# Four filler memsets of the logits, moved ahead of the logits in a column-normalised attention with a soft mixture of experts

## The chip, the cores and the metric

The kernel runs on one core of one Trainium2 chip. The metric is the device time of one execution in microseconds (us), as the median of the runs.

## The reference, cut to what matters

q, k and v are 4 batches of 5056 rows by 256 columns, all float32.

```python
qn = q / (np.linalg.norm(q, axis=1, keepdims=True) + 1e-06)
kn = k / (np.linalg.norm(k, axis=1, keepdims=True) + 1e-06)
s = kn.transpose(0, 2, 1) @ qn / tau          # 256 x 256 for each batch
a = softmax(s, axis=-1)
x = (v @ a).reshape(20224, 256)
logits = x @ phi                              # 20224 rows, 32 slots
d = softmax(logits, axis=0)                   # over all rows
slot_input = d.T @ x                          # 32 x 256
slot_out = relu(slot_input @ w1[e]) @ w2[e]   # 8 experts, 4 slots each
out = softmax(logits, axis=1) @ slot_out
```

## The kernel before

The core has four engines that compute: TensorE (PE) multiplies matrices into PSUM, which has eight banks (here S0, S1, T0, T1, LB, GB, X0, X1); VectorE (DVE) and ScalarE (ACT) read and write PSUM and SBUF; GpSimd (POOL) does little here. All loads and stores are issued by SyncE (SP), in one queue. Each engine works through its own list of instructions in order, and waits for others by semaphores.

**The attention, in steps of 512 rows.** A step u (0 to 39, ten for each batch) loads 512 rows of q and k into the tile `raw` (five buffers). ACT squares them (`sq`, L206) and makes a rounded copy (`hl`, `cast`, L185); DVE computes the rounding's remainder (`low`, L191) and adds up the squares (L212). PE adds the products of k and q to two banks (`S`, L227, L233, L234). When a batch is done, ACT and DVE take `S` out (`shi` L242, `ssb` L247), DVE folds the sums of squares (`att_sums`, L251), PE adds them over the partitions (`nn`, L257), DVE copies the result (`rn`, L262), and the softmax follows. The result, multiplied by `phi`, is `M`, 256 by 32.

**The logits, in pieces of 1024 rows of v.** A piece p (0 to 19, five for each batch) is loaded as `v` and transposed (`vt`, by a second load or by PE as `vTp` and an ACT copy). `logits(p, lb)` multiplies `vt` by `M` into the bank `lb` as the tile `L`: 128 partitions by 8 groups of 32 slots (L390). ACT copies `L` to `lt` (L412, `logit_copy`), DVE takes its maxima (`mxs`, L418) and a 32 by 32 transpose (`nat`, L422). After each group of three or two pieces the running maximum is found: PE turns it (`rp`, L433), DVE reduces it to one row (`row` L439, `rowrun` L442 or L444), PE spreads it over the partitions again (`cp`, L448), DVE copies it out (`negm`, L453), ACT takes the exponential of `lt` (L469), DVE transposes that to `dn` (L479), and PE gathers `dn` times `v` (`G`, L499). The pieces of one batch are worked on while PE and DVE are in the attention steps of the next batch.

**The filler.** A batch has 5056 rows and its last piece (p = 4, 9, 14, 19) only 960. Of its eighth group of rows the upper 64 partitions have no data. They are set to a large negative number, so that maxima and sums pass over them; the matmuls of that piece leave them alone:

```python
        if q == PB - 1:
            dve.memset(L[HD:, 7, :], -1e30)
```

This memset is inside `logits`, so it stands on DVE at the place where the step `logits` has in the list, and the first matmul of that step waits for it.

**The order.** Each piece of work is a step: `at(key, f, ...)` and `tail(...)` append it to a plan, and the table `ORDER` lists the numbers of the steps in the order in which they are emitted. It sets the order on every engine and in SP's queue. A tile that takes over a bank or a buffer waits for the last users of the tile that had it before.

Of the kernel before, what the change touches and what calls it, by code (L numbers as in the profile page):

```python
# [16 lines left out]
P, S, G = 128, 32, 4  # L17
UB = 10
PB = 5
# [9 lines left out]


ORDER = [
# [47 lines left out]
]  # L79


# [1 line left out]
def colnorm_attention_soft_moe(  # L83
# [27 lines left out]
    def bank(i, name):  # L111
        return ps.tile([P, 512], F32, tag=f"b{i}", name=name)
# [264 lines left out]
    XT = {17: sqtag[NU - 2], 18: sqtag[NU - 1], 19: sqtag[NU - UB]}  # L377
    Ls = {}

    def logits(p, lb):  # L380
        b, q = divmod(p, PB)
        M = st[b]["M"]
        L = bank(lb, f"L{p}")[:, : 8 * S].rearrange("p (j s) -> p j s", s=S)
        if q == PB - 1:
            dve.memset(L[HD:, 7, :], -1e30)
        for m in range(2):
            x = vts[p, m].rearrange("p (j w) -> p j w", w=P)
            for g in range(G):
                n = 7 if q == PB - 1 and g >= 2 else 8
                pe.matmul(  # L390
                    L[S * g : S * g + S, :n, :],
                    M[:, m, :],
                    x[:, :n, S * g : S * g + S],
                    start=m == 0,
                    stop=m == 1,
                )
        Ls[p] = L

    def group(p):
        b, q = divmod(p, PB)  # L400
# [356 lines left out]
        else:  # L757
            sp.dma_start(oa[b, p][:, hf], o2[:, hf])

    def wake(k):  # L760
        w = bank(X0, "wake")
        for _ in range(k):
            pe.matmul(w[:, :P], ones, ones, start=True, stop=True)

# [44 lines left out]
    for p in range(14):  # L809
        k = FV + 2 * p  # L810
        k += 0.5 if k % UB == UB - 1 else 0
        at(k, logits, p, (LB, T1)[p % 2])
        at(k + 0.25, logit_copy, p)
        at(k + 0.40, logit_max, p)
# [89 lines left out]
    for m in range(2):  # L904
        tail(0.35 + 0.3 * m, att_join, 3, m)
        tail(0.4 + 0.3 * m, att_scale, 3, m)
        tail(0.6 + 0.3 * m, att_exp, 3, m)
        tail(2.5 + 0.6 * m, att_turn, 3, m)
    tail(0.5, logits, 14, LB)
    tail(2.3, logit_max, 14)  # L910
    tail(2.3, logit_nat, 14)
# [21 lines left out]
    chain(2.8, 2, gl, 1)  # L933
    ts = {15: (5.3, S0), 16: (6.2, S1), 17: (9.1, LB), 18: (17.0, S0), 19: (18.0, S1)}
    for p, (t, lb) in ts.items():
        tail(t, logits, p, lb)
        tail(t + 1.0, logit_copy, p)
        tail(t + 1.0, logit_max, p)
        tail(t + (1.1 if p < 17 else 3.0), logit_nat, p)
# [133 lines left out]
```

## Time and profile before

| what | value |
|---|---|
| median of 3 runs | 295.02 us (294.59 to 295.24) |
| the profiled execution's own time | 296.7 us |
| its span, from the first instruction to the last | 294.8 us |
| busy: DVE, PE, ACT | 239.4, 255.5, 185.6 us |
| instructions: DVE, PE, ACT | 396, 2296, 268 |
| moved by DMA | 115.59 MB, 392 GB/s over the span |
| mean granted TensorE clock | 0.952 of 2.4 GHz |

The busy times are sums over the whole span; the ends of matmuls are modelled, so a busy PE is not PE at its peak. The profiled execution's time is 1.9 us more than its span; those 1.9 us lie before the first and behind the last instruction that the profile has.

### The profile page before, as it was taken

To read this page: it belongs to the slowest core of one execution; us is meant where nothing else is said; L and a number is where in the kernel's file an instruction comes from. 1 tells how busy PE (TensorE), PEld (TensorE's weight loads), DVE (VectorE), ACT (ScalarE), POOL (GpSimd) and SP (SyncE) were. 2 spreads that over 40 slices of the span, in tenths; PEclk is the share of its full clock that TensorE was granted. 3 is DMA by queue.
4 is the path that set the end of the run, shared out by engine and by line. 5 is a ranking of instruction groups with operands and counts; after the bars stand their busy time and mean duration, and the time that the engine had idled before them with its cause. 6 is when DMAs were issued, how large, how long until landed. Compare 5 with 4: busy or idle time off the path is not lost.

```text
span 294.8 us, 5824 instructions
## 1 busy us (share of the span) xinstructions
PE 255.5 (87%) x2296; PEld 196.3 (67%) x2296; DVE 239.4 (81%) x396; ACT 185.6 (63%) x268; POOL 5.6 (2%) x10
## 2 busy tenths in 40 slices
PE   5789999999989999997999999899999999986000
PEld 3679878878858888774877777566553778755000
DVE  1399999999999899999799999979975769996100
ACT  2898879968887876867657986146442435864200
POOL 0000001000001000000200000010000000000000
PEclk9999999999997999999999999999997999999555
DMA  7999999999999789999989999999999939999996
GB/s 253 411 422 414 422 424 421 418 425 403 403 396 391 271 311 419 417 423 422 425 328 399 412 414 421 420 420 422 418 415 418 412 133 385 412 417 421 420 427 275
DMA packets 23067, 115.59 MB, mean 392 GB/s; under 512 B 2688, under 2 KB 2688, under 8 KB 15104
## 3 DMA queue, kind: packets, MB, share of 16 engines
q1 hardware_dynamic: 23040, 115.22, 96.3%
q8 instruction: 18, 0.29, 0.4%
q14 instruction: 9, 0.07, 0.1%
HBM read 94.24 MB, written 20.97 MB: 391 GB/s over the span
## 4 chain that ended last, share of the span: by engine, by line
PE 42%; DVE 23%; DMA 15%; issue 9%; ACT 5%; SPq 1%; ACTq 0%; DVEq 0%
DVE sq L212 12%; PE S L227 11%; PE S L233 6%; DMA w<-in_moe_w_dram 6%; DVE hl L191 5%; PE G L499 5%; DMA out_dram<-o 5%; PE L L390 4%; DMA raw<-in_qk_dram 3%; PE S L234 3%; PE op L726 2%; PE op_None L726 2%; PE O L687 2%; DMA v<-in_v_dram 2%; PE vTp L368 2%
## 5 line engine op out<-in xcount | busy, mean ns | idle before, releaser
L227 PE MATMUL S<-raw 128*128 128x256 f32 (+1 forms) x328 | 85.2, 396 | 6.1 <-DMA raw<-in_qk_dram 5.7
L212 DVE TENSOR_TENSOR sq<-sq,sq 128x1024 f32<-128x1024 f32 (+1 forms) x63 | 84.9, 1368 | 1.4 <-ACT sq L206 0.8
L206 ACT ACTIVATE sq<-raw 128x2048 f32<-128x2048 f32 x40 | 76.1, 1913 | 13.6 <-DMA raw<-in_qk_dram 6.0
L227 PEld LDWEIGHTS S<-raw 128*128 128x128 f32 (+1 forms) x328 | 59.8, 195 | 17.8 <-DMA raw<-in_qk_dram 7.3
L233 PE MATMUL S<-hl 128*128 128x512 f32 x156 | 65.1, 447 | 0.6 <-DVE hl L191 0.6
L191 DVE TENSOR_TENSOR hl<-raw,hl 128x1024 fp32r<-128x1024 f32 x39 | 47.2, 1216 | 10.1 <-ACT hl L185 10.1
L234 PE MATMUL S<-hl 128*128 128x256 f32 x156 | 43.8, 281 | 0.0
L185 ACT CAST hl<-raw 128x1024 fp32r<-128x1024 f32 x39 | 40.1, 1044 | 5.8 <-PE S L234 2.0
L233 PEld LDWEIGHTS S<-hl 128*128 128x128 f32 x156 | 29.5, 189 | 9.2 <-issue 2.4
L234 PEld LDWEIGHTS S<-hl 128*128 128x128 f32 x156 | 29.6, 190 | 0.8
L750 DVE COPY o<-op_None 128x512 f32<-128x512 f32 x30 | 18.8, 681 | 7.5 <-DMA out_dram<-o 6.4
L748 ACT COPY o<-op_None 128x512 f32<-128x512 f32 x30 | 15.9, 593 | 12.2 <-DMA out_dram<-o 7.3
L499 PE MATMUL G<-v,dn 128*32 128x256 f32 (+1 forms) x320 | 23.3, 382 | 0.0
L726 PE MATMUL op_None<-so,cT 32*128 32x256 f32 x240 | 18.8, 397 | 2.6 <-DVE o L750 1.6
L390 PE MATMUL L<-vt,M 128*32 128x256 f32 (+1 forms) x272 | 17.4, 380 | 4.1 <-issue 2.8
L726 PEld LDWEIGHTS op_None<-so,cT 32*128 32x128 f32 x240 | 14.8, 184 | 6.2 <-PE op_None L726 3.1
L499 PEld LDWEIGHTS G<-v,dn 128*32 128x32 f32 (+1 forms) x320 | 11.8, 109 | 7.2 <-issue 1.8
L390 PEld LDWEIGHTS L<-vt,M 128*32 128x32 f32 x272 | 8.4, 109 | 10.2 <-issue 4.2
L368 PE MATMUL vTp<-ident,v 128*128 128x128 f32 x96 | 14.8, 280 | 0.0
L368 PEld LDWEIGHTS vTp<-ident,v 128*128 128x128 f32 x96 | 11.9, 145 | 2.5 <-issue 0.7
L412 ACT COPY lt<-L 128x256 f32<-128x256 f32 x20 | 7.1, 372 | 9.7 <-DVE mxs L418 5.2
L375 ACT COPY vt<-vTp 128x512 f32<-128x512 f32 (+1 forms) x18 | 10.5, 581 | 3.6 <-PE vTp L368 3.6
(113 smaller groups left out, 264.2 us busy)
## 6 DMA issues: line engine op xcount, KB each, us to landing
raw<-in_qk_dram SPq DMA_DIRECT2D x39, 1024.0 KB, 8.8
v<-in_v_dram SPq DMA_DIRECT2D x40, 512.0 KB, 8.7
out_dram<-o SPq DMA_DIRECT2D x15, 1024.0 KB, 13.2
vt<-in_vt_dram SPq DMA_DIRECT2D x21, 512.0 KB, 8.6
w<-in_moe_w_dram SPq DMA_DIRECT2D x8, 1024.0 KB, 12.2
w<-in_moe_w_dram SPq DMA_DIRECT2D x16, 512.0 KB, 10.0
out_dram<-o SPq DMA_DIRECT2D x10, 512.0 KB, 4.6
vt<-in_vt_dram SPq DMA_DIRECT2D x4, 480.0 KB, 9.3
```

Source lines behind the costliest of these rows:

```text
L185: act.copy(hl[:, :ns, 0::2, :], raws[u][:, :ns])
L191: dve.tensor_tensor(hl[:, :ns, 1::2, :], raws[u][:, :ns], hl[:, :ns, 0::2, :].bitcast(F32), op=ALU.subtract)
L206: act.activation(sq, raws[u], AF.Square)
L212: dve.tensor_tensor(a[:, lo:hi], a[:, lo:hi], s[:, lo:hi], op=ALU.add)
L227: pe.matmul(sm[:, :C], raw[:pc, j, 1, cols], raw[:pc, j, 0, :], start=first, stop=False, skip_group_check=True)
L233: pe.matmul(sm, hl[:, j, 2, cols], rhs, start=first, stop=False, skip_group_check=True)
L234: pe.matmul(sm[:, :C], hl[:, j, 3, cols], hl[:, j, 0, :], start=False, stop=False, skip_group_check=True)
L368: pe.transpose(tp[:, n : n + pc], vs[p][:pc, 4 * h + jj, P * m : P * m + P], ident[:pc, :pc])
L390: pe.matmul(L[S * g : S * g + S, :n, :], M[:, m, :], x[:, :n, S * g : S * g + S], start=m == 0, stop=m == 1,)
L499: pe.matmul(gp[S * g : S * g + S, :C], dn[:pc, x, j, :], vt[:pc, j, :], start=x == 0 and j < G, stop=x == n - 1 and j >= G,)
L726: pe.matmul(ops[b, p, hf, g][:, h, :], cT[b][S * g : S * g + S, 4 * i : 4 * i + 4, :].rearrange("s j t -> s (j t)"), so[S * g : S * g + S] ...
L750: dve.tensor_copy(dst, src)
```

## The change

The memset becomes a step of its own, `logit_fill`, which also takes the bank; `logits` takes the bank itself only where no such step did. The four new steps are put into the plan, and `ORDER` has each of them 10 to 14 places ahead of the `logits` of the same piece. Every number in the table at or above the first new step's is shifted by one for each new step below it; apart from that the order of the other steps is the same. `wake` gets a second parameter that no call uses.

```diff
+    def logit_bank(p, lb):
+        Ls[p] = bank(lb, f"L{p}")[:, : 8 * S].rearrange("p (j s) -> p j s", s=S)
+
+    def logit_fill(p, lb):
+        logit_bank(p, lb)
+        dve.memset(Ls[p][HD:, 7, :], -1e30)
+
     def logits(p, lb):
         b, q = divmod(p, PB)
         M = st[b]["M"]
-        L = bank(lb, f"L{p}")[:, : 8 * S].rearrange("p (j s) -> p j s", s=S)
-        if q == PB - 1:
-            dve.memset(L[HD:, 7, :], -1e30)
+        if p not in Ls:
+            logit_bank(p, lb)
+        L = Ls[p]
...
-        Ls[p] = L
...
         k += 0.5 if k % UB == UB - 1 else 0
+        if p % PB == PB - 1:
+            at(k - 0.9, logit_fill, p, (LB, T1)[p % 2])
         at(k, logits, p, (LB, T1)[p % 2])
...
+    tail(0.4, logit_fill, 14, LB)
     tail(0.5, logits, 14, LB)
...
     for p, (t, lb) in ts.items():
+        if p % PB == PB - 1:
+            tail(t - 0.1, logit_fill, p, lb)
         tail(t, logits, p, lb)
```

Of the table one line of each kernel, with the step of the filler of p = 4 (434) and that of its logits (434 before, 435 now):

```diff
-    188, 627, 387, 165, 557, 421, 187, 184, 628, 416, 388, 422, 561, 423, 559, 558, 630, 194, 562, 175, 429, 434,
+    188, 629, 387, 165, 559, 421, 187, 434, 184, 630, 416, 388, 422, 563, 423, 561, 560, 632, 194, 564, 175, 429,
```

In the rows below a name's first number is the piece, step or batch and the number behind the last underscore that of the buffer; DMAHW is a load, Activation is ACT, and a wait for DVE on DVE, or for PE on PE, is for an earlier instruction of the same engine.

**VectorE at the first filler (p = 4, at the turn from batch 1 to batch 2 of the attention).** Before:

```order
L191 TENSOR_TENSOR hl20_670<-raw20_655,hl20_670 128x4x256 [waits DMAHW6_49,Activation_49]
L422 STREAM_TRANSPOSE nat0_112<-L1_545 128x256
L251 TENSOR_TENSOR sq10_340<-sq10_340 128x1024
L439 TENSOR_REDUCE row0_0_706<-rp0_0_703 1x32 [waits PE_49]
L442 COPY rowrun_118<-row0_0_706 1x128 [waits DVE_49]
L247 TENSOR_TENSOR ssb1_710<-shi1_692,S1_0_371 128x256 [waits Activation_49]
L251 TENSOR_TENSOR sq10_340<-sq10_340 128x512
L385 MEMSET L4_728 64x32
L247 TENSOR_TENSOR ssb1_710<-shi1_692,S1_1_372 128x256 [waits Activation_49]
L191 TENSOR_TENSOR hl21_714<-raw21_664,hl21_714 128x4x256 [waits DMAHW0_49,Activation_49]
```

Now:

```order
L192 TENSOR_TENSOR hl20_670<-raw20_655,hl20_670 128x4x256 [waits DMAHW6_49,Activation_49]
L386 MEMSET L4_697 64x32 [waits DVE_49]
L429 STREAM_TRANSPOSE nat0_112<-L1_545 128x256
L252 TENSOR_TENSOR sq10_340<-sq10_340 128x1024
L446 TENSOR_REDUCE row0_0_708<-rp0_0_705 1x32 [waits PE_49]
L449 COPY rowrun_118<-row0_0_708 1x128 [waits DVE_49]
L248 TENSOR_TENSOR ssb1_712<-shi1_692,S1_0_371 128x256 [waits Activation_49]
L252 TENSOR_TENSOR sq10_340<-sq10_340 128x512
L248 TENSOR_TENSOR ssb1_712<-shi1_692,S1_1_372 128x256 [waits Activation_49]
L192 TENSOR_TENSOR hl21_716<-raw21_664,hl21_716 128x4x256 [waits DMAHW0_49,Activation_49]
```

The memset has moved up past six instructions, to just behind `hl20`, and waits there only for earlier work of DVE itself.

**VectorE at the second filler (p = 9, at the turn from batch 2 to batch 3).** Before:

```order
L428 TENSOR_REDUCE mx1_0_1189<-mxs1_0_1069 128x1 [waits DVE_49]
L251 TENSOR_TENSOR sq20_681<-sq20_681 128x512 [waits DVE_49]
L191 TENSOR_TENSOR hl30_1164<-raw30_1072,hl30_1164 128x4x256 [waits DMAHW6_49,Activation_49]
L608 TENSOR_SCALAR cs0_1108<-cs0_1108 128x40
L609 RECIPROCAL cs0_1108<-cs0_1108 128x40 [waits DVE_49]
L439 TENSOR_REDUCE row1_0_1205<-rp1_0_1199 1x32 [waits PE_49]
L444 TENSOR_TENSOR rowrun_118<-rowrun_118,row1_0_1205 1x128 [waits DVE_49]
L247 TENSOR_TENSOR ssb2_1210<-shi2_1191,S2_0_750 128x256 [waits Activation_49]
L551 COPY acc_116<-sp0_1186 32x256
L385 MEMSET L9_1213 64x32 [waits Activation_49]
L247 TENSOR_TENSOR ssb2_1210<-shi2_1191,S2_1_751 128x256 [waits Activation_49]
L453 COPY negm1_0_1243<-cp1_0_1241 128x1 [waits PE_49]
```

Now:

```order
L435 TENSOR_REDUCE mx1_0_1189<-mxs1_0_1069 128x1 [waits DVE_49]
L252 TENSOR_TENSOR sq20_681<-sq20_681 128x512 [waits DVE_49]
L386 MEMSET L9_1195 64x32 [waits Activation_49]
L192 TENSOR_TENSOR hl30_1164<-raw30_1072,hl30_1164 128x4x256 [waits DMAHW6_49]
L615 TENSOR_SCALAR cs0_1108<-cs0_1108 128x40
L616 RECIPROCAL cs0_1108<-cs0_1108 128x40 [waits DVE_49]
L446 TENSOR_REDUCE row1_0_1207<-rp1_0_1201 1x32 [waits PE_49]
L451 TENSOR_TENSOR rowrun_118<-rowrun_118,row1_0_1207 1x128 [waits DVE_49]
L248 TENSOR_TENSOR ssb2_1212<-shi2_1191,S2_0_750 128x256
L558 COPY acc_116<-sp0_1186 32x256
L248 TENSOR_TENSOR ssb2_1212<-shi2_1191,S2_1_751 128x256 [waits Activation_49]
L460 COPY negm1_0_1243<-cp1_0_1241 128x1 [waits PE_49]
```

The memset has moved up past seven instructions, ahead of `hl30`, and it has taken its wait for ACT along: the bank that `L9` takes was that of `L7`, which ACT copies to `lt` (L412). The waits for ACT of `hl30` and of the first `ssb` are gone, being covered by the memset's.

**TensorE at the same place** (further matmuls of the same tiles are left out). Before:

```order
L433 MATMUL rp1_0_1199<-ident_90,mx1_0_1189 1x128 [waits DVE_49]
L390 MATMUL L9_1213<-vt9_0_1172,M1_1003 32x256 [waits DMAHW5_49,DVE_49,PE_49]
L390 MATMUL L9_1213<-vt9_1_1147,M1_1003 32x256 [waits DMAHW3_49]
L390 MATMUL L8_1224<-vt8_0_1126,M1_1003 32x256 [waits DMAHW2_49]
L390 MATMUL L8_1224<-vt8_1_1162,M1_1003 32x256 [waits Activation_49]
L448 MATMUL cp1_0_1241<-negone_97,rowrun_118 128x1 [waits PE_49]
L257 MATMUL nn2_1248<-ones_95,sq20_681 128x1 x4
L227 MATMUL S3_0_1254<-raw30_1072 128x256 [waits DMAHW6_49]
```

Now:

```order
L440 MATMUL rp1_0_1201<-ident_90,mx1_0_1189 1x128 [waits DVE_49]
L398 MATMUL L9_1195<-vt9_0_1172,M1_1003 32x256 [waits DMAHW5_49,DVE_49,PE_49]
L398 MATMUL L9_1195<-vt9_1_1147,M1_1003 32x256 [waits DMAHW3_49]
L398 MATMUL L8_1224<-vt8_0_1126,M1_1003 32x256 [waits DMAHW2_49]
L398 MATMUL L8_1224<-vt8_1_1162,M1_1003 32x256 [waits Activation_49]
L455 MATMUL cp1_0_1241<-negone_97,rowrun_118 128x1 [waits DVE_49,PE_49]
L258 MATMUL nn2_1248<-ones_95,sq20_681 128x1 [waits DVE_49]
L258 MATMUL nn2_1248<-ones_95,sq20_681 128x1 x3
L228 MATMUL S3_0_1254<-raw30_1072 128x256 [waits DMAHW6_49]
```

The order of the matmuls is the same. The first of `L9` still waits for DVE, now for the memset at its new place; `cp` and `nn`, which came behind a matmul that had waited for a later DVE instruction, now have waits for DVE of their own, on `rowrun` and on the folded squares.

At the third filler (p = 14) the memset moves up past six DVE instructions and waits for no other engine, and at the fourth (p = 19) it moves up past four and waits for ACT's copy of `L16`, whose bank it takes.

## Rows read from the trace of the kernel before

**Rows 1.** The page: the engines' busy time; GB/s in 40 slices of the span.

```profile
PE 255.5 (87%) x2296; PEld 196.3 (67%) x2296; DVE 239.4 (81%) x396; ACT 185.6 (63%) x268; POOL 5.6 (2%) x10
...
GB/s 253 411 422 414 422 424 421 418 425 403 403 396 391 271 311 419 417 423 422 425 328 399 412 414 421 420 420 422 418 415 418 412 133 385 412 417 421 420 427 275
```

**Rows 2.** The chain that ended last: start us, us, what ("issue" is waiting).

```profile
85.84 0.84 issue
...
137.49 1.93 issue
```

**Rows 3.** What DVE waited for, 80 to 170 us: total us, times, longest.

```profile
DVE negm L453 <- PE cp L448: 2.0, 1, 2.0
DVE ssb L296 <- PE rq L289: 1.1, 1, 1.1
```

**Rows 4.** Timeline, first filler: start us, us, what, [idle before <- releaser].

```profile
85.80 0.67 DVE L251 TENSOR_TENSOR sq<-sq 128x512 f32<-128x512 f32 x1
...
86.49 0.09 DVE L385 MEMSET L<- 64x32 f32 x1
...
86.68 1.06 PE L390 MATMUL L<-vt,M 128*32 128x256 f32 x16 [0.84 <-issue]
...
88.89 1.72 PE L227 MATMUL S<-raw 128*128 128x256 f32 x4
89.06 0.16 DVE L262 COPY rn<-nn 128x4 f32<-128x4 f32 x1 [1.04 <-PE nn L257]
```

**Rows 5.** Timeline, second filler.

```profile
133.97 0.37 ACT L412 COPY lt<-L 128x256 f32<-128x256 f32 x1 [4.07 <-DVE mxs L418]
...
135.74 0.69 DVE L251 TENSOR_TENSOR sq<-sq 128x512 f32<-128x512 f32 x1
...
136.35 1.22 DVE L191 TENSOR_TENSOR hl<-raw,hl 128x1024 fp32r<-128x1024 f32 x1
...
136.87 0.39 ACT L412 COPY lt<-L 128x256 f32<-128x256 f32 x1
...
138.27 0.28 DVE L444 TENSOR_TENSOR rowrun<-rowrun,row 1x128 f32<-1x128 f32 x1
...
139.23 0.09 DVE L385 MEMSET L<- 64x32 f32 x1
...
139.42 1.92 PE L390 MATMUL L<-vt,M 128*32 128x256 f32 x32 [1.94 <-issue]
...
141.27 0.38 PE L448 MATMUL cp<-negone,rowrun 1*128 1x1 f32 x2
...
141.68 0.16 DVE L453 COPY negm<-cp 128x1 f32<-128x1 f32 x1 [2.05 <-PE cp L448]
...
142.49 2.84 PE L227 MATMUL S<-raw 128*128 128x256 f32 x12
```

**Rows 6.** Timeline, third filler.

```profile
186.24 1.13 PE L499 MATMUL G<-v,dn 128*32 128x256 f32 x16
...
188.42 0.09 DVE L385 MEMSET L<- 64x32 f32 x1
...
188.56 1.06 PE L390 MATMUL L<-vt,M 128*32 128x256 f32 x16 [1.20 <-DVE L L385]
...
189.73 1.20 DVE L191 TENSOR_TENSOR hl<-raw,hl 128x1024 fp32r<-128x1024 f32 x1
...
192.20 0.16 DVE L262 COPY rn<-nn 128x4 f32<-128x4 f32 x1 [0.60 <-PE nn L257]
```

**Rows 7.** Timeline, fourth filler.

```profile
209.41 0.37 ACT L412 COPY lt<-L 128x256 f32<-128x256 f32 x1 [1.83 <-DVE nat L422]
```

**Rows 8.** Stretches: us, busy of each engine, granted clock, DMA share, GB/s.

```profile
86.00:89.00 3.00, 2.32 (x27) 1.81 (x28) 2.02 (x4) 1.83 (x2) 0.00 (x0) 1.00 1.01 416
89.00:93.00 4.00, 4.00 (x14) 3.31 (x14) 3.90 (x8) 3.29 (x4) 1.01 (x1) 0.57 1.02 415
```

**Rows 9.** What SP's queue waited for, 82 to 112 us.

```profile
SPq L121 <- PE S L227: 18.9, 5, 7.4
```

More of the change, by code (lines that the diff above doesn't have):

```diff
@@ L758, in store, with wake @@
             sp.dma_start(oa[b, p][:, hf], o2[:, hf])
-    def wake(k):
-        w = bank(X0, "wake")
+    def wake(k, tb=X0):
+        w = bank(tb, "wake")
         for _ in range(k):
```

91 rows, old and new, of the table ORDER are left out of this document.

## The prediction

> **What bounds the kernel now.** I read the page first. Over the span PE is busy for 87%, and the loads run at 400 to 425 GB/s in most slices, with dips to 271, 311 and 328 GB/s in slices 14, 15 and 21 [rows 1]. A slice is 7.4 us, so the dips lie at 96 to 111 us and 147 to 155 us. No single engine carries the span, and the place has to be looked at by itself.
>
> The chain of waits comes next. Through the middle of the span it runs mostly on PE, and it holds two long pieces in which PE waits for nothing that the profile names: 0.84 us at 85.84 and 1.93 us at 137.49 [rows 2]. The timeline says what stands there. At 86.49 and at 139.23 DVE runs the filler memset, and PE's next matmul, `L`, starts 0.19 us later each time [rows 4, 5]. PE's order at the second place shows that this matmul waits for DVE. The same happens at 188.42, where the profile does name the memset as the releaser of a PE wait of 1.20 us [rows 6]. At the fourth filler PE does not wait for it, since it has `L18` to do first.
>
> Last the list of waits on DVE, from 80 to 170 us. The two longest entries are 2.0 us for `cp` and 1.1 us for `rq` [rows 3]; the wait of 1.04 us for `nn` is in the timeline [rows 4]. The waits for `cp` and `nn` lie just behind the two fillers: PE waits for DVE's memset, and then DVE waits for PE. Between these places DVE has hardly a gap, so what the change gives is what DVE gets of its own idle time there, more than what PE gets.
>
> **The first filler (p = 4).** DVE's work at 85.80 ends at 86.47, the memset at 86.58, `L4` starts at 86.68 [rows 4]. Now the memset stands six instructions earlier, behind `hl20`, and `L4` can start when `L3` is out, 0.84 us earlier. Behind it stand `cp` (needs `rowrun`, long done) and `nn` (needs the squares folded by 86.47, and reaches PE at about 87.1). Both move by the whole 0.84 us, and so does the S matmul of 88.89. DVE waited 1.04 us for `nn` until 89.06, so it takes all 0.84 us and still waits 0.2. The memset, 0.09 us, is only moved. **Term: 0.84 us.**
>
> **The second filler (p = 9).** PE waited 1.94 us, until 139.42 [rows 5]. Here the memset carries a wait for ACT's copy of `L7`, which ends at 136.87 + 0.39 = 137.26. DVE comes to the memset at 135.74 + 0.69 = 136.43, so it now stands still for some 0.85 us and starts `hl30` at about 137.35 instead of 136.35. Queued behind it on DVE are `hl30`, the two `cs`, `row`, `rowrun` and the two `ssb`, all about 1.0 us later; `rowrun`, which ended at 138.27 + 0.28 = 138.55, is what PE's `cp` then waits for. On PE `L9` starts at about 137.5, `L9` and `L8` take 141.27 - 139.42 = 1.85 us, to 139.4; `cp` waits for `rowrun` until 139.6 and `nn` follows; the S matmul starts at about 140.8 instead of 142.49, 1.67 us earlier. On DVE the second `ssb` ends at about 140.5, `cp` is already there, and `negm` starts at 140.5 instead of 141.68. So DVE gets back 1.18 us of its 2.05 us of idle time, and loses the rest to the new wait. I take DVE's figure, rounded, because DVE is dense afterwards. **Term: 1.15 us.** The bounds are 0, if the copy of `L7` is late by as much as the gain, and PE's 1.67 us.
>
> The Trainium skill, PSUM — Partial Sum Buffer, section "Engine vs sequencer instructions", says that the queues of ScalarE, VectorE and GpSimd are strictly first in, first out. By that rule nothing behind the memset can pass it while it waits for ACT, which is the 1.15 us above; if `hl30` could pass it, the term would be the whole 2.05 us. The rule speaks against moving a memset ahead of its bank's last reader, and no row of before shows this very wait.
>
> **The third filler (p = 14).** PE's gather ends at 186.24 + 1.13 = 187.37, and `L14` starts at 188.56 [rows 6]. The memset now stands six DVE instructions earlier and waits for no other engine. PE then does `L14`, the gather of piece 11 and the S matmuls of `hl38` and `hl39` about 1.1 us earlier; the last of these are held by the remainder of `hl39`, which DVE finishes at 189.73 + 1.20 = 190.9. DVE waited 0.60 us for `nn` before 192.20. From there to the end the chain goes through PE and short DVE pieces, so I take PE's value. **Term: 1.1 us,** bounds 0 (if the loads have become the limit here, where GB/s shows no dip) and 1.2.
>
> **The fourth filler (p = 19).** ACT's copy of `L16` waited for a transpose of DVE just ahead of the memset's new place, and then took 0.37 us, to 209.78 [rows 7]. DVE now waits there for most of that copy, and `cT`, `negm` and with it ACT's exponentials are later by up to 0.3 us, less the 0.09 us that fall away behind them. PE has `L18` to do meanwhile. **Term: -0.1 us,** bounds -0.3 and 0.
>
> **What follows the moved work.** No load changes its place in SP's queue. In the first dip that queue waits five times for PE's S matmuls, 18.9 us in all, to free `raw` buffers [rows 9]; earlier S matmuls issue those loads earlier and fill the dips. The two dips hold about (420-271 + 420-311 + 420-328)/420 x 7.4 = 6 us of load time, more than the 2 us that the first two terms ask of them.
>
> **The sum.** 0.84 + 1.15 + 1.1 - 0.1 = 3.0 us. The span goes from 294.8 to 291.8 us and the profiled execution's own time from 296.7 to 293.7. The median, 295.02 us, is 1.7 us below that execution, and I take the same 3.0 us from it: **292.0 us.** With all terms at their ends the sum lies between 0.5 us (0.84, 0, 0, -0.3) and, with the clock below, 4.8 us (0.84 + 1.1, 1.67, 1.2, 0).
>
> **Rivals.** *The clock comes along.* Right after the first pause and the narrow matmuls of `nn`, the granted clock falls: 1.00 from 86 to 89 us, a mean of 0.57 from 89 to 93 [rows 8]; 0.43 x 4.0 = 1.7 us of PE's time is lost to the 1.2 GHz level. Without the pause PE has wide matmuls in its place, and the clock might stay at 2.4 GHz. For: the fall follows on the pause. Against: after the longer pause at 137.49 PE goes on at 2.4 GHz, with 12 S matmuls in 2.84 us where 4 took 1.72 us after the first [rows 4, 5], so the pause alone does not decide. DVE could then also take its 1.1 us wait for `rq` [rows 3]: 295.02 - 4.1 = 290.9 us.
>
> *Half of it is eaten.* The copy of `L7` is ACT's and need not move with DVE, and the loads from 155 us on run without a dip. If only the first place pays, plus a little, the time is 294.0 us.
>
> *The loads set the time.* Then earlier compute only waits for data, and nothing changes: 295.0 us. For: 33 of the 40 slices are above 390 GB/s [rows 1]. Against: SP's queue waits for PE in the dips, and in the list of DVE's waits no load appears. The Trainium skill, Perfetto Trace Analysis, section "Roofline", gives about 435 GB/s as the most that one core's DMA engines move; the trace agrees, with 427 GB/s in its best slice. As an estimate from that page 115.59 MB would take 266 us, so by it the loads are the nearest bound.
>
> *The new wait costs more than it saves.* At the second filler everything on DVE hangs on one ACT copy. It breaks even there when the copy ends at 136.43 + 2.05 = 138.5, 1.2 us later than now, and turns the whole change when it ends another 1.8 us later, at 140.3: then ACT would have to be late by 3.0 us, a square and a cast. If it ends at 141.3, the time is 296.0 us. Against: ACT works without a gap from 133.97, where it had waited 4.07 us for DVE's maxima [rows 5], so it moves with DVE.
>
> **How the numbers follow.** Chances: the forecast 0.58 (its own range 291.0 to 293.3, where the third term may fail), the clock 0.12, half eaten 0.12, the loads 0.10, the new wait 0.08. What a measurement of this kernel can tell from no change is about 0.2%, 0.6 us. Faster by more: the forecast, the clock and most of "half eaten", 0.80. Within: the loads and the rest of "half eaten", 0.12. Slower: 0.08. The range goes from 290.2, below the clock's case and near the sum of the upper ends, to 295.0, which leaves out the new wait and half of the loads' case.
>
> **What would show it.** In the profile of the changed kernel the two unnamed waits of PE before `L` and the named one are gone; `L4` follows `L3` at once; DVE's wait for `nn` at the first place is about 0.2 us; at the second place DVE has a wait for ACT's `lt` of 0.8 to 0.9 us before the memset and none of 2 us before `negm`; `nn` of the last batch ends about 1.1 us earlier against its surroundings; the dips in GB/s are shallower. I am wrong if DVE's new wait is as long as the old one, if the dips stay as deep while PE waits for `raw`, or if the clock falls at another place.

## The result, and the profile after

The changed kernel takes **291.32 us** (median of 5 runs, 291.13 to 291.69); the kernel before took 295.02 us (median of 5, 293.66 to 295.25). The medians are 3.7 us apart; the ratio is 0.9881, interval 0.9845 to 0.9917. The forecast was 292.0 us. Executions more than 1.5% above the fastest of their kernel, two of before and one each of `after3` and `late4`, are left out of the ratios and mean spans below.

The page of the profiled execution of after (span 289.3 us, own time 291.13 us, mean granted clock 0.958) answers to [rows 1]:

```profile
PE 255.1 (88%) x2296; PEld 196.9 (68%) x2296; DVE 238.8 (83%) x396; ACT 185.8 (64%) x268; POOL 5.6 (2%) x10
...
GB/s 221 414 425 412 425 423 418 417 429 407 423 420 415 342 348 418 418 425 420 423 421 417 410 414 419 418 424 418 421 416 419 401 178 386 413 421 423 423 421 280
```

The engines work as long as before, in a span 5.5 us shorter. The dips of 271 and 311 GB/s have become 342 and 348, and the third (328) is gone.

The timeline at the first place, beside [rows 4]:

```profile
84.73 1.89 PE L398 MATMUL L<-vt,M 128*32 128x256 f32 x29
...
87.94 0.16 DVE L263 COPY rn<-nn 128x4 f32<-128x4 f32 x1
```

The memset stands at 83.36 now. `L3` and `L4` are one row of 32 matmuls, of which the profile lists the last 29 together, without a gap, and DVE comes to `rn` without a wait. At the second place, beside [rows 5]:

```profile
134.07 0.39 ACT L419 COPY lt<-L 128x256 f32<-128x256 f32 x1
...
134.54 1.21 DVE L192 TENSOR_TENSOR hl<-raw,hl 128x1024 fp32r<-128x1024 f32 x1 [0.91 <-DMA raw<-in_qk_dram]
134.54 0.09 DVE L386 MEMSET L<- 64x32 f32 x1
...
134.73 1.92 PE L398 MATMUL L<-vt,M 128*32 128x256 f32 x32
...
136.86 0.35 PE L455 MATMUL cp<-negone,rowrun 1*128 1x1 f32 x2 [0.21 <-DVE rowrun L451]
...
137.64 0.14 DVE L460 COPY negm<-cp 128x1 f32<-128x1 f32 x1
```

DVE's 2.05 us ahead of `negm` are gone. A new wait of 0.91 us stands ahead of the memset and `hl30`, whose rows both start at 134.54. The profile names a load for it; ACT's copy of `L7` ends at 134.07 + 0.39 = 134.46, just ahead. At the third place [rows 6] the gather and `L14` join, and `rn` has no wait:

```profile
182.09 1.14 PE L506 MATMUL G<-v,dn 128*32 128x256 f32 x16
182.98 1.11 PE L398 MATMUL L<-vt,M 128*32 128x256 f32 x16
...
187.31 0.14 DVE L263 COPY rn<-nn 128x4 f32<-128x4 f32 x1
```

DVE's waits from 80 to 170 us [rows 3] begin with this new one, and the next is of 0.3 us; SP's queue from 82 to 112 us [rows 9] waits 15.1 us for PE's S matmuls instead of 18.9:

```profile
DVE hl L192 <- DMA raw<-in_qk_dram: 0.9, 1, 0.9
```

The two stretches behind the first place [rows 8] lie at 85 to 88 and 88 to 92 us now, and both are at the 2.4 GHz level:

```profile
85.00:88.00 3.00, 3.00 (x40) 2.28 (x33) 2.88 (x7) 2.75 (x2) 0.00 (x0) 1.00 0.99 412
88.00:92.00 4.00, 4.00 (x23) 3.51 (x23) 3.96 (x8) 3.40 (x4) 1.01 (x1) 1.00 1.05 421
```

So two things were open: why 3.7 us between medians and 5.5 us between the two profiled executions (294.8 and 289.3 us), and which filler gave what.

### The profile page after: what moved, and what is told of

The parts are those of the page before. It is cut to its first block, busy times and chain, and to the rows that moved or that the text cites. A ratio compares the mean times of both kernels' runs of the same rounds, so it can differ in the third digit from the quotient of the medians.

```text
span 289.3 us, 5823 instructions
## 1 busy us (share of the span) xinstructions
PE 255.1 (88%) x2296; PEld 196.9 (68%) x2296; DVE 238.8 (83%) x396; ACT 185.8 (64%) x268; POOL 5.6 (2%) x10
## 4 chain that ended last, share of the span: by engine, by line
DVE 40%; PE 27%; issue 12%; DMA 7%; ACT 7%; SPq 1%; ACTq 0%; DVEq 0%
DVE sq L213 19%; DVE hl L192 8%; DMA out_dram<-o 5%; PE S L228 4%; PE G L506 3%; PE H L663 3%; DMA raw<-in_qk_dram 3%; ACT sq L207 3%; PE op L733 3%; PE S L234 2%; PE op_None L733 2%; PE O L694 2%; PE L L398 2%; DVE mxs L425 1%; DVE nat L604 1%
## 5 line engine op out<-in xcount | busy, mean ns | idle before, releaser
L228 PEld LDWEIGHTS S<-raw 128*128 128x128 f32 (+1 forms) x328 | 60.5, 197 | 16.7 <-DMA raw<-in_qk_dram 5.6
```

The costliest lines, as they stand in the source:

```text
L228: pe.matmul(sm[:, :C], raw[:pc, j, 1, cols], raw[:pc, j, 0, :], start=first, stop=False, skip_group_check=True)
```

## The experiments

All kernels keep the instructions of after. Only the list of steps is changed before it is emitted; `put` takes a filler out and sets it directly ahead of another step, or `behind` places further:

```diff
-    for x in ORDER:
-        key, _, f, a = plan[x]
-        f(*a)
+    steps = [(f, a) for _, _, f, a in (plan[x] for x in ORDER)]
+
+    def put(p, g, *ga, behind=0):
+        fill = next(s for s in steps if s[0] is logit_fill and s[1][0] == p)
+        steps.remove(fill)
+        at_ = next(i for i, s in enumerate(steps) if s[0] is g and s[1][: len(ga)] == ga)
+        steps.insert(at_ + behind, fill)
...
+    for f, a in steps:
+        f(*a)
```

### All four back, and one at a time

```diff
+    put(4, logits, 4)
+    put(9, logits, 9)
+    put(14, logits, 14)
+    put(19, logits, 19)
```

`none` has these four lines; `only4`, `only9`, `only14` and `only19` each leave out the line of the filler that they are named after. `after2` and `after3` are the changed kernel again.

> All four fillers stand directly ahead of their logits again; the helper functions stay, and the instructions are those of the kernel before. Every theory expects 295.0 us. What it is for is the clock: the profiled execution of before has a mean granted clock of 0.952 and a stage at the 1.2 GHz level right after the first pause; the kernel after has 0.958 and no such stage there. Theory 'terms' (each place gives back what DVE loses there, and no more): in most timed executions of this order the clock is near 0.957 too, the stage is a feature of some executions, and their span is 1.5 us below the profiled one of before (294.8 us). Rival 'clock': the pause makes the stage each time, all executions show about 0.952 and their spans stand near 293.1 us with it.

> Only the filler of p = 4 stands ahead, the other three directly ahead of their logits. Theory 'terms': 0.85 to 1.1 us below before, ratio 0.9964 to 0.9971; PE's 0.84 us ahead of L4 is gone, and the waits at the other places are as before. Rival 'clock': the stage at the 1.2 GHz level behind the first pause goes too, and this alone gives 2.0 to 2.7 us, ratio 0.991 to 0.993, so that the other places hold little more than 1 us together. Rival 'half eaten': what the first place gives is lost again at the second turn, where DVE waits longer for cp; ratio 0.999 to 1.000.

> Only the filler of p = 9 stands ahead. Theory 'terms': 1.15 to 1.3 us below before, ratio 0.9956 to 0.9961; at the second place DVE waits 0.8 to 0.9 us for ACT's copy of L7 ahead of the memset and no longer 2 us for cp. Rival 'new wait': DVE's new wait eats the gain, ratio 0.999 to 1.001. Rival 'the loads': the gain is lost at the next load that DVE or PE waits for, ratio 0.999 to 1.000.

> Only the filler of p = 14 stands ahead. Theory 'terms': 1.1 to 1.3 us below before, ratio 0.9956 to 0.9963; PE's named wait of 1.2 us for the memset is gone and DVE's 0.6 us for nn with it. Rival 'the loads': from 155 us on the loads have no dip and set the time, so that the last batch ends where it ended, ratio 0.999 to 1.000. Theory 'terms' also has the three single gains and the fourth's 0 to -0.1 us add up to what the whole change gives, 3.7 us within 0.5; rival 'half eaten' has them add up to more than that.

> The changed kernel again, with the same instructions. The first runs of single fillers showed that executions of one and the same program differ by a stage of 3.4 us at the 1.2 GHz level, which some have and some have not, and by some 1.7 us with it: a mean granted clock of 0.961 to 0.963 goes with no such stage ahead of the last one, 0.955 to 0.958 with one, 0.951 to 0.953 with two. Theory 'terms': the change is worth 3.5 us at an equal number of stages, so that executions with one stage have spans of 289.5 us (before: 293.1 us) and any without have 287.9 us (before: 291.4 us). Rival 'clock': the change makes its gain by the clock, so executions without a stage, if there are any, have the same span as before's, or the gap at an equal clock is below 2 us.

> The changed kernel once more, as the neighbour of the runs below on the same chip: span 287.5 us in executions without a stage at the 1.2 GHz level ahead of the last one (mean clock 0.961 and above), 289.5 us with one (0.955 to 0.958).

> Only the filler of p = 19 stands ahead, the other three directly ahead of their logits. By the prediction's fourth term this is 0.1 us slower than before, between 0 and 0.3: spans of 291.5 us without a stage at the 1.2 GHz level ahead of the last one, 293.2 us with one and 295.0 us with two, ratio 0.999 to 1.002. A rival, that PE's pauses at the other places are shortened by anything that this step moves, would show a span 0.5 us or more below before's at an equal clock; nothing in the profile speaks for it.

**The clock first.** `none` came out as before: 294.85 us against 294.79, ratio 1.0005 (0.9972 to 1.0038). But its profiled execution has a span of 291.8 us where that of before had 294.8, with the same instructions. The windows of the stretch behind the first place say why, before first, then `none`:

```profile
89.25:92.65 3.40, 3.40 (x13) 2.76 (x11) 3.37 (x7) 2.94 (x4) 1.01 (x1) 0.50 1.04 422
```

```profile
89.25:92.65 3.40, 3.40 (x20) 2.98 (x20) 3.37 (x7) 3.06 (x4) 1.01 (x1) 1.00 1.02 400
```

PE is busy throughout in both; at the 1.2 GHz level it gets 13 matmuls done, at 2.4 GHz 20. In the traces such stretches stand at two places: here, and between 215 and 226 us, from the first matmuls of `H` on or from the narrow ones (32 columns) just ahead of them. In the last three of its 40 slices every trace is at the 1.2 GHz level; that is not counted. Traces with none of them have a mean clock of 0.961 to 0.963, with one 0.956 to 0.958, with two 0.951 or 0.952, so the clock listed for each execution tells how many it had, taken to the nearest of these values. Mean spans in us by that, with the number of executions:

| kernel | none | one | two |
|---|---|---|---|
| before | 291.45 (21) | 293.21 (34) | 294.89 (10) |
| `none` | 291.63 (3) | 293.07 (7) | 294.95 (2) |
| `only4` | 290.40 (7) | 292.04 (5) | |
| `only9` | 289.78 (5) | 292.00 (5) | |
| `only14` | 290.23 (6) | 291.88 (6) | |
| `only19` | 291.40 (2) | 292.82 (8) | 294.45 (2) |
| after, `after2`, `after3` | 287.35 (4) | 289.45 (11) | 291.0 (1) |

At an equal number the change gives 4.1, 3.8 and 3.9 us. From one column to the next is 1.4 to 2.2 us, and 1.7 to 1.8 in the row of before, which has most executions. Of the five traces with the pause of 0.84 us at the first place only that of before has a stretch there, and none of the eight without the pause has. Over all executions the mean number of stretches is the same in before (0.87, of 67) and in after (0.88, of 17), so the counts give no sign that the change gains by having fewer. The profiled execution of before had two and that of after one, which is 1.7 of the 5.5 us.

**Then the places.** The eight copies and maxima `rowrun` stand on DVE between the fillers: the first ahead of the first filler's gap, the second behind it, the fourth behind the second's, the sixth behind the third's, the eighth behind the fourth's. From the timelines, the time in us from one to the next, in traces that are at 2.4 GHz throughout up to the eighth (that of before is not: its half-clock stretch makes the first two 17.27 and 50.15, which is 1.4 and 0.3 us more than in `none`, 1.7 us together):

| kernel | 1st to 2nd | 2nd to 4th | 4th to 6th | 6th to 8th |
|---|---|---|---|---|
| `none` | 15.90 | 49.83 | 43.52 | 17.76 |
| `only4` | **14.86** | 49.84 | 43.50 | 17.76 |
| `only9` | 15.89 | **48.50** | 43.52 | 17.75 |
| `only14` | 15.90 | 49.82 | **42.22** | 17.75 |
| `only19` | 15.89 | 49.84 | 43.50 | **17.68** |
| after | 14.86 | 48.50 | 42.22 | 17.68 |
| `after2` | 14.86 | 48.49 | 42.19 | 17.67 |

Each filler shortens its own stretch, and no other stretch moves by more than 0.02 us. The gains are 1.04, 1.33, 1.30 and 0.08 us one at a time, 3.75 in all, and 1.04, 1.34, 1.33 and 0.09 together, 3.80. Nothing of them is given back before the eighth `rowrun`. The ratios of medians (`only4` 0.9933, 0.9901 to 0.9964; `only9` 0.9930, 0.9895 to 0.9965; `only14` 0.9933, 0.9903 to 0.9963; `only19` 0.9988, 0.9957 to 1.0020) make each of the first three some 2 us, since more of those executions than of before's were without a half-clock stretch (18 of 34 against 21 of 65); whether that is chance is not shown. `after2` (0.9867, 0.9817 to 0.9918) and `after3` (0.9838, 0.9781 to 0.9894) repeat the result.

### The wait at the second filler

`behind9` sets the second filler behind `hl30`, `early9` ahead of the last fold of the squares; `copy7` moves ACT's copy instead; `copy7_19` is `copy7` with the fourth filler put back.

```diff
+    put(9, low, 30, behind=1)
+    put(19, logits, 19)
```

That is `behind9`, and this `early9`:

```diff
+    put(9, att_sums, 2, 1)
```

`copy7` moves another step; `find` gives a step's position in the list:

```diff
+    step = steps.pop(find(logit_copy, 7))
+    steps.insert(find(cast, 31), step)
```

> As after, but the filler of p = 9 stands one DVE instruction later, just behind hl30, and that of p = 19 directly ahead of its logits. Ahead of hl30 the memset waited 0.91 us for ACT's copy of L7; behind it the wait should be hidden by hl30. Theory 'PE is the limit there': L9 cannot start before 134.7 us anyway, since PE is busy until then; it now starts at about 135.1, and only the waits of cp (0.21 us) and nn (0.23 us) can go, so the result is after within 0.4 us at an equal clock. Rival 'DVE is the limit there': the whole 0.91 us come back and the span is 0.8 to 0.9 us below after's at an equal clock.

> As after, but the filler of p = 9 stands one DVE instruction earlier, ahead of the last fold of the squares (0.69 us). The memset's wait for ACT's copy of L7 can only grow, from 0.91 us to about 1.6, and the fold now comes behind it. Theory 'the wait is for ACT': hl30 and all behind it start 0.6 us later than in after, and the span is 0.5 to 0.7 us above after's at an equal clock; the profile still names a load at this wait, though no load moves. Rival 'the wait is for the load' that the profile names: the fold does its 0.69 us anyway, hl30 starts where it did, and the time is that of after.

> As after, but ACT copies L7 one step earlier, ahead of the cast of hl31 instead of behind it and one half of shi; DVE's and PE's orders are those of after. The copy ends at about 133.3 us instead of 134.46, before DVE comes to the memset at 133.6. Theory 'the wait is for ACT': DVE's 0.91 us at the memset are gone; PE's L9 starts where it did, since PE is busy until 134.7, and only the waits of cp and nn go (0.21 and 0.23 us): 0.2 to 0.5 us below after at an equal clock. Rival 'the wait is for the load' that the profile names: the wait stays and the time is that of after. Rival 'DVE is the limit there': 0.8 to 0.9 us below after.

> As copy7 (ACT copies L7 ahead of the cast of hl31, all else as in after), and the filler of p = 19 directly ahead of its logits again. In copy7's trace the wait of DVE at the memset is gone, and so are those of cp and nn; DVE's negm and PE's first S matmul of the next batch come some 0.8 us earlier against the work ahead of them. Theory 'DVE is the limit there': 0.8 to 0.9 us below after at an equal clock, 286.6 us without a stage and 288.6 us with one. Theory 'PE is the limit there', on record for copy7: 0.2 to 0.5 us below. The filler of p = 19 changes nothing that can be measured by either.

| kernel | 2nd to 4th `rowrun` | 6th to 8th | span, none | span, one | ratio to before |
|---|---|---|---|---|---|
| `after2` | 48.49 | 17.67 | 287.45 (2) | 289.43 (4) | 0.9867 |
| `behind9` | 48.19 | 17.98 | 287.77 (3) | 288.90 (3) | 0.9845 (0.9801 to 0.9889) |
| `early9` | 49.09 | 17.67 | 288.45 (2) | 290.10 (3) | 0.9895 (0.9846 to 0.9945) |
| `copy7` | 47.69 | 17.67 | 287.40 (3) | 288.60 (3) | 0.9834 (0.9790 to 0.9879) |
| `copy7_19` | 47.68 | 17.74 | 286.88 (5) | 289.1 (1) | 0.9802 (0.9758 to 0.9847) |

**It is ACT that DVE waits for.** In `copy7` no load moves, and the wait that the profile had put down to a load is gone. Its timeline of ACT, and of DVE:

```profile
132.45 0.38 ACT L419 COPY lt<-L 128x256 f32<-128x256 f32 x1
```

```profile
132.53 0.69 DVE L252 TENSOR_TENSOR sq<-sq 128x512 f32<-128x512 f32 x1
133.18 1.25 DVE L192 TENSOR_TENSOR hl<-raw,hl 128x1024 fp32r<-128x1024 f32 x1
133.23 0.09 DVE L386 MEMSET L<- 64x32 f32 x1
```

In `early9` the fold has come behind the memset, and the wait, 1.56 us, stands ahead of both. My expectation that a load would be named there again was wrong: no releaser is named.

```profile
134.58 0.67 DVE L252 TENSOR_TENSOR sq<-sq 128x512 f32<-128x512 f32 x1 [1.56 <-issue]
134.59 0.09 DVE L386 MEMSET L<- 64x32 f32 x1
```

The fold needs nothing of ACT and still stood behind the memset; `early9` loses 49.09 - 48.49 = 0.60 us by it. The Trainium skill, PSUM — Partial Sum Buffer, section "Engine vs sequencer instructions", says that VectorE's queue is strictly first in, first out; the fold's 1.56 us agree.

**What the wait costs.** `behind9` hides it behind `hl30`, but then PE comes to `L9` late, and DVE waits 0.40 us for `cp`; it gains 0.30 us there, as "PE is the limit" had it. It loses 0.31 us again between the sixth and the eighth `rowrun`. Some 0.08 of it is the fourth filler, which `behind9` puts back as well. The rest may be a wait for a load: its list of PE's waits, 190 to 197 us, has one that those of `after2`, `copy7` and `copy7_19` don't have:

```profile
PE vTp L369 <- DMA v<-in_v_dram: 0.3, 1, 0.3
```

`copy7` lets both engines start early and gains 0.80 us between these two `rowrun`, which that theory did not have: it took PE to be busy until `L9`, where PE's listed row only seemed to reach that far. By the intervals "DVE is the limit" holds for `copy7`. In the spans it is 0.0 to 0.9 us, with few executions on either side; the beginning of the kernel alone, up to the first `rowrun`, differs by 0.6 us between these executions (85.07 in `after2`, 84.49 in `copy7_19`). `copy7_19` has the shortest median of all, 288.86 us against 291.17 for `after3` beside it, but five of its six executions had no half-clock stretch; at an equal number the two differ by 0.4 and 0.2 us, which is the range of "PE is the limit". So the 0.8 us are shown at this place; how much of them reaches the end of the kernel is not.

### The pause made longer

`late4` is after with the first filler behind the second `ssb` and `hl21`.

```diff
+    for g in ((att_join, 1, 1), (low, 21), (logit_fill, 4)):
+        step = steps.pop(find(*g))
+        steps.insert(find(logits, 4), step)
```

> The opposite of the change at the first place: the filler of p = 4 stands behind the second ssb and hl21, 1.2 us further back on DVE than in the kernel before; the other three are as in after. PE's pause ahead of L4 grows from 0.84 to about 2.2 us. Theory 'the pause is paid in full': the first place costs its 1.05 us (only4) and another 1.4 us, so that the span is 2.4 us above after's at an equal clock, 289.9 us without a stage and 291.9 us with one. Rival 'it is made up for later' (the loads set the pace, or DVE's slack): half of that or less, at most 1.2 us above after. Rival 'the pause brings the stage': nearly all executions have one stage more than after's.

The ratio to before is 1.0041 (1.0006 to 1.0076). PE waits 2.31 us ahead of `L4`, and DVE waits for `nn` in turn:

```profile
90.64 0.16 DVE L263 COPY rn<-nn 128x4 f32<-128x4 f32 x1 [2.49 <-PE nn L258]
```

From the first `rowrun` (85.44) to `rn` are 5.20 us; in `none` it is 88.94 - 85.20 = 3.74 us and in after 87.94 - 85.24 = 2.70 us. So the place costs 2.50 us more than in after; with two stretches the spans are 293.57 us (3 executions) against 291.0 us (one). The pause is paid in full, and the rival "made up for later" falls. The third theory is borne out too: of all 12 executions 8 have a clock of 0.947 or less, below that of two stretches, 3 have 0.950 or 0.951 and one 0.958. In the profiled one the clock is at 0.50 right behind the pause again:

```profile
90.75:94.10 3.35, 3.35 (x11) 2.71 (x11) 3.32 (x8) 2.81 (x4) 1.01 (x1) 0.50 1.00 406
```

## Why the prediction was right, and where it was off

The mechanism was right at the first three places, which make nearly all of the gain; at the fourth a wait of PE was overlooked. The sum, 3.0 us, was 0.7 to 0.8 us short of the 3.7 us between medians and the 3.75 to 3.80 us in the traces.

**First filler: 0.84 us forecast, 1.04 measured.** The term took PE's idle time as the profile lists it. It is too short by what two rows of matmuls give up when they become one. The rows for this were there before: 16 matmuls of `L` take 1.06 us [rows 4] and 32 in one row 1.92 us [rows 5], so a gap between two rows costs 2 x 1.06 - 1.92 = 0.20 us beside its listed length. 0.84 + 0.20 is the 1.04 us that was found. The Trainium skill, TensorE: Matmul & The Clock Gate, section "Step-by-step: what each phase is for", says that in a stream the drain of one matmul overlaps the filling of the next; the trace agrees: 13 matmuls of `L3` and the 16 of `L4` took 1.02 and 1.06 us before, and the same 29 in one row take 1.89, 0.19 us less. The row of the 13 in before:

```profile
84.81 1.02 PE L390 MATMUL L<-vt,M 128*32 128x256 f32 x13
```

**Second: 1.15 forecast, 1.33 measured.** DVE's new wait was forecast at some 0.85 us and is 0.91; the old one of 2.05 us is gone, as forecast. The difference, 1.14 us, is the term. Of the other 0.2 us 0.12 is DVE's own work, which takes 46.92 us of this stretch in `none` and 46.80 in `only9`; the rest is not traced to a row. DVE's figure was nearer than PE's 1.67.

**Third: 1.1 forecast, 1.30 measured.** PE's named wait of 1.20 us [rows 6] had a hidden part too: from the start of the gather to that of `L14` were 188.56 - 186.24 = 2.32 us, and now 182.98 - 182.09 = 0.89, 1.43 us less. What DVE had to take of it was more than its 0.60 us ahead of `rn`. Behind that stood another wait for PE in before, which the prediction does not list and of which 0.13 us are left in after, where this row starts at 189.76 and the one ahead of it ends at 189.63:

```profile
195.20 0.42 DVE L247 TENSOR_TENSOR ssb<-shi,S 128x256 f32<-128x256 f32 x1 [0.72 <-PE S L227]
```

The two waits give 0.60 + 0.59 = 1.19 us, and DVE's own work in the stretch is 0.11 us shorter (41.60 us in `none`, 41.49 in `only14`). The measured gain lies above the upper bound of 1.2 that I gave, since that bound was a listed idle time.

**Fourth: -0.1 forecast, +0.08 measured.** The sign was wrong. The intervals show the gain three times: 0.08 in `only19`, 0.09 in `after2` and, the other way, 0.07 from `copy7` to `copy7_19`. The cost was there: from the seventh `rowrun` to the `negm` behind it are 1.47 us in `only19` and 1.24 us in `none`. What the term had wrong is that PE does not wait for this filler. The profile lists `L18` and `L19` of before as one row, but it takes 2.15 us, where 32 matmuls in one row take 1.92 [rows 5]; with the filler moved it takes 1.92 as well. So 0.23 us of waiting were hidden in this row:

```profile
209.76 2.15 PE L390 MATMUL L<-x,M 128*32 128x256 f32 x32 [0.25 <-DVE nat L422]
```

That these 0.23 us are what gives the cost back is argued, not shown.

**The rivals.** "Half eaten" and "the loads" fall: each gain is kept. "The new wait" has its price, 0.8 us at its own place if `copy7` is the measure, but the change saves more than it costs. "The clock comes along" named the right rows and is not what the gain came from: the stretch comes and goes in executions of the same program, and at an equal number of them the change is worth 3.8 to 4.1 us. Two of 17 executions of after still have two. In the one that has a trace (`after3`) both lie at 215 to 222 us, so whether the first place became rarer with the change is open. That a longer pause brings more of them is shown by `late4`.

**What would show it.** The waits before `L` and `negm` are gone, the new one is there, the dips are shallower. The clock falls at no place where it did not fall before: after has one stretch, at 217 to 220 us, and before had one there too, at 222 to 226. DVE's wait for `nn` at the first place, forecast at 0.2 us, is nil: 1.04 us of wait took 1.04 us of gain.

## What to carry to other kernels

An instruction that another engine waits for, and that needs little itself, belongs where its inputs are ready; but on an in-order engine it brings its own waits to the new place, and all that stands behind pays them. So look for what it waits for there, and see whether that can move as well: in `copy7` it brought the work behind it forward by 0.8 us, though how much of it reaches the end is open. Price a pause of PE from start to start, not by the idle time listed, and compare two profiled executions only after their granted clocks have been compared.

## What was not expected

One program ran at three levels: before's executions have spans of 291.5, 293.2 and 294.9 us, by whether PE fell to 1.2 GHz for none, one or two stretches ahead of the kernel's end. Where they lay is known only for the executions that were profiled. This spread, 3.4 us, is nearly as large as the whole gain. And a wait of DVE for ACT was listed once as a wait for a load and once with no releaser at all.
